# Top-32 attention and a leaky-ReLU block: the softmax division moved from the weights to the transposed values

## The chip, the cores and the metric

The kernel runs on one core of one Trainium2 chip. The metric is device time in microseconds of one execution; smaller is better. Before the change it is 1467.62 us, the median of three runs (1466.69 to 1473.15).

The engines have short names in the profile: PE is TensorE's matmul and PEld its weight load, DVE is VectorE, ACT is ScalarE, POOL is GpSimd, SP is SyncE, which here only issues DMAs. Each engine works through its own instructions in order and waits at semaphores for the others.

## The reference

The shapes are 8 batches, 8 heads, 576 positions, head size 64, all float32; then 4608 tokens, model width 512, hidden width 2048.

```python
scores = scale * np.matmul(q, k.transpose(0, 1, 3, 2))
kth = np.partition(scores, -32, axis=-1)[..., -32:-31]
scores = np.where(scores >= kth, scores, -1e9)
attn = np.exp(scores - np.max(scores, axis=-1, keepdims=True))
attn = attn / (np.sum(attn, axis=-1, keepdims=True) + 1e-09)
x = matmul(attn, v) laid out as (tokens, heads * head size)
h = x @ w_in
out = np.maximum(0.01 * h, h) @ w_out
```

## The kernel before, in words

**Units and steps.** Attention is cut into 144 units. A whole unit is 128 query rows of one pair of heads; its scores are a tile `s_sb` of 128 x 2 x 576 (row, head of the pair, key). Because 576 is 4 x 128 + 64, there are also left units: 64 rows of two pairs of heads each. The main loop (L742) runs over steps `s`; step `s` finds the top 32 of unit `s` on DVE and does the later stages of the units before it. DVE's work for a unit (`top_k`, L295) is two L302 instructions (pairwise maxima and minima), eight L307 (`max`, eight largest at a time) and six L312 (`match_replace`), and is issued in slots between the other engines' work.

**What a unit goes through.** PE computes scores for the two units of steps `s + 2` and `s + 3` at the end of every even step (`scores`, L214) into two PSUM tiles `wide` and one `narrow`, and ACT copies them to `s_sb` (L238, four copies). After the unit's top 32, `limits` (L316) makes two small vectors on ACT and POOL (L322 to L324), `mask` (L326) and `exponents` (L330) run on ACT, two instructions each, in place; the exponentials add up their row sums `z`. `sums` (L334) adds 1e-9 on ACT, `reciprocals` (L338) takes the reciprocal on DVE, between two slots of the next unit's rounds, and `normalize` (L342) multiplies the weights by it on ACT, in place. All of this is in step `n + 1` for unit `n`.

**Transposing.** In step `n + 2`, `transpose` (L345) splits the float32 weights into their two 16-bit halves on POOL (L352, two copies), stores each half to DRAM (L353) and reads both back with one transposing DMA (L355) into `wT`, of which there are three. For units named in `HASTY` (the first eight, 14 and 15), PE transposes nine blocks instead (L365), and ACT copies them out (L371), also in step `n + 2`.

**Values.** `weigh_whole` (L394, 40 matmul instructions for two units) and `weigh_left` (L406) multiply V by `wT`. `values_at` (L622) says when: the two units of a pair of steps together, in the middle of step `(n|1) + 3`, or one step earlier for hasty ones. The result is already transposed: rows are head size, columns are tokens. `keep_values` (L413) copies it with ACT (L418) to the tiles `x`, of which two sets exist.

**The second block.** Tokens go through it in chunks: two of 128 (chunks 0 and 1, `plain`, L573) and 17 of 256 (`mlp`, L491). A chunk of 256 takes 8 steps to become ready. For each, PE makes `ph` (L510) in eight groups, ACT applies the leaky ReLU to `gT` (L516), and PE makes seven products `pz` (L526), with sums and differences of blocks on POOL (L467) that stand in for an eighth product; ACT copies the results to `o_sb` (L533). Two PSUM tiles `ml` serve all of it.

**The order around the change.** Everything is issued in an order written out by hand in the loop at L742. The chunk's work is a generator; `mlp_steps(budget)` (L601) runs it seven times a step until the budget is used up. A matmul's cost is its number of columns. `slot_budget` (L648) divides the work that is waiting by the slots until the step at which the next chunk becomes ready. `sum_now` (L465) issues waiting sums on POOL, `send_now` (L472) stores results through SP. SP's queue holds, in order: loads of Q, K and V, stores of results, and for each unit the two stores and the transposing DMA. `KEPT` names twelve units whose scores are computed in the first steps (`keep_scores`, L273), stored to DRAM and fetched later. Before the loop, the weights, stored as float64, are rounded to float32 on the chip (some 60 us).

Of the kernel before, what the change touches and what calls it, by code (L numbers as in the profile page):

```python
# [9 lines left out]
F32 = mybir.dt.float32  # L10
# [10 lines left out]
def kernel(  # L21
# [192 lines left out]
    def scores(us):  # L214


        narrow = ps_sc.tile([P, 2, 512], F32, name="narrow")
        ps = {}
        for k, u in enumerate(us):
            wide = ps_sc.tile([P, 2, 512], F32, name="wide", bufs=2)  # L220
            ps[u] = ((wide[:, :, 0:WIDE], 0, WIDE),
                     (narrow[:, :, k * NARROW:(k + 1) * NARROW], WIDE, S))

        order = ((us[0], 0), (us[0], 1), (us[1], 1), (us[1], 0))
        for u, part in order:
            to, k0, k1 = ps[u][part]
            for n in range(0, len(u.quarters), 4):
                for i, pi, side, r0, q0 in u.quarters[n:n + 4]:
                    qt, kt = qk_of[pi]
                    d = slice(side * D, (side + 1) * D)  # L230
                    nc.tensor.matmul(to[r0:r0 + LEFT, i, :], qt[d, q0:q0 + LEFT],  # L231
                                     kt[d, k0:k1], start=True, stop=True)
        for u in us:
            u.both = work.tile([P, 2, S], F32, name="s_sb", bufs=5)
            u.s = [u.both[:, i, :] for i in range(2)]
        for u, part in order:
            to, k0, k1 = ps[u][part]
            nc.scalar.copy(u.both[:, :, k0:k1], to)  # L238
# [77 lines left out]
    def limits(u):  # L316
# [4 lines left out]
        u.z = small.tile([P, 2], F32, name="z")  # L321
# [12 lines left out]
    def sums(u):  # L334
        u.ze = small.tile([P, 2], F32, name="ze")
        nc.scalar.activation(u.ze, u.z, AF.Copy, bias=1e-9, scale=1.0)

    def reciprocals(u):  # L338
        u.rz = small.tile([P, 2], F32, name="rz")
        nc.vector.reciprocal(u.rz, u.ze)  # L340

    def normalize(u, i):  # L342
        nc.scalar.activation(u.s[i], u.s[i], AF.Copy, bias=0.0, scale=u.rz[:, i:i + 1])  # L343
# [69 lines left out]
    def keep_values(pair, po, b, q0):  # L413
        ch, col = x_at(b * S + q0)
        if ch not in x_of:
            x_of[ch] = [xpool.tile([P, CHMAX], F32, name=f"x{c}") for c in range(HP)]
        for side in range(2):
            nc.scalar.copy(x_of[ch][pair % HP + side][:, col:col + po.shape[-1]], po[:, side, :])  # L418
# [6 lines left out]
    def hidden_of_few(ch, x):  # L425

        g_of = {}
        for j in range(NFC // 4):
            ph = ps_ml.tile([P, 512], F32, name="ph", tag="ml")
            for c in range(HP):  # L430
                nc.tensor.matmul(ph, x[c][:, 0:P], w_in[c][:, j * 512:(j + 1) * 512],  # L431
                                 start=(c == 0), stop=(c == HP - 1))
                if c == 1:
                    yield 2 * 512
# [56 lines left out]
    def mlp(ch):  # L491
# [13 lines left out]
        for f0 in range(HALF):  # L505
            ph = ps_ml.tile([P, 2, CHMAX], F32, name="ph", tag="ml")
            for i in range(2):
                f = f0 + i * HALF
                for c in range(HP):
                    nc.tensor.matmul(  # L510
                        ph[:, i, 0:n], w_in[c][:, f * P:(f + 1) * P], x[c][:, 0:n],
# [107 lines left out]
    HASTY = (*range(8), 14, 15)  # L619
    MIDDLE, END = 0, 1  # L620

    def values_at(n):  # L622

        return (n | 1) + LAG - (n in HASTY), MIDDLE

# [3 lines left out]
    EARLY_SCORES = {0: 4, 1: 2, 2: 1, 3: 2, 4: 1, 5: 2}  # L629
# [12 lines left out]
    def attended(*place):  # L642
# [5 lines left out]
    def slot_budget(s):  # L648
# [5 lines left out]
        return backlog[0] / ((until + 1 - s) * SLOTS)  # L654

    EARLY_SHARE = 500
    SLOTS = 7

    with tc.manual_schedule():
# [65 lines left out]
        def values(*place):  # L725
# [3 lines left out]
            po = ps_sc.tile([P, 2, 512], F32, name="wide", bufs=2)  # L729
# [7 lines left out]
        def keep(weighed, *place):  # L737
            for u, po in weighed:
                keep_values(u.pairs[0], po, u.b, u.q0)
            attended(*place)  # L740

        for s in range(len(steps) + LAG + 1):  # L742
            assert s < 7 or not to_keep
            cur, old, older, new = unit(s), unit(s - 1), unit(s - 2), ()
            in_haste = s - 2 in HASTY
# [10 lines left out]
            slot()  # L756
            load_waiting()
            send_now()
            if old:
                limits(old)  # L760
            if older and not in_haste:
                transpose(older)
# [3 lines left out]
            if older and in_haste:  # L766
                transpose_in_haste(older)
            if old:
                mask(old, 1)
            slot()  # L770
            if older and in_haste:
                keep_transposed(older)
            mlp_steps(budget)
            if old:
                exponents(old, 0)
            weighed = values(s, MIDDLE)
            if old:
                exponents(old, 1)
                sums(old)
            keep(weighed, s, MIDDLE)  # L780
            if s == 7:
                sum_weights()
            sum_now(3)
            mlp_steps(budget)
            slot()
            if s % 2:
                slot()
            if old:
                reciprocals(old)
            mlp_steps(budget)  # L790
            if old:
                normalize(old, 0)
                normalize(old, 1)
            mlp_steps(budget)
            slot()
            slot()
            if unit(s + 3) in early_units:
                fetch_scores(unit(s + 3))
            mlp_steps(budget)
            if new:  # L800
                scores(new)
            score_early(EARLY_SCORES.get(s, 0))
            budget = slot_budget(s + 1)
            mlp_steps(budget)
# [64 lines left out]
```

## Time and profile before

| what | value |
|---|---|
| median of three runs | 1467.62 us |
| the profiled execution's own time | 1463.53 us |
| its span, first to last instruction | 1461.8 us |
| busy: PE / PEld | 1373.3 us (94%) / 1065.6 us (73%) |
| busy: DVE / ACT / POOL | 1317.9 us (90%) / 1058.5 us (72%) / 728.6 us (50%) |
| DMA | 232.19 MB in 384,445 packets, 320,944 of them under 512 B |
| mean granted clock of TensorE | 0.982 |

The span is what the views below divide. A view by groups gives, for a line and an operation, the count, the busy time, the mean duration of one, and the idle time before it with what ended it. A view of waits sums the idle time by who waited for whom. The chain of waits follows back from the last instruction through whatever released each step. A view by stretches gives busy time per engine in a window of the span. PE's matmuls overlap in the pipeline: the mean duration of one L510 matmul is 383 ns, but 40 of them in a row take 8.83 us, 0.22 us each.

### The profile page before, as it was taken

The numbers are of one execution on the slowest core, as the hardware profiler recorded it, in microseconds if no ns is written. First come the engines' busy times: TensorE is split into PE (matmuls) and PEld (weight loads), VectorE is DVE, ScalarE is ACT, GpSimd is POOL, SyncE is SP. The second block draws the span as 40 slices with busy tenths as digits, with TensorE's granted clock in tenths as the row PEclk, the third lists the DMA queues.
The fourth block names the chain that finished last, engine by engine and source line by source line (L and its number), as shares of the span: only waits on it lengthen the run. The fifth ranks groups of instructions, "written<-read, shape, count | busy, mean of one in ns | idle before, by whom it ended". The sixth has DMA issues, their size and how long they took to land.

```text
span 1461.8 us, 27967 instructions
## 1 busy us (share of the span) xinstructions
PE 1373.3 (94%) x9848; PEld 1065.6 (73%) x9850; DVE 1317.9 (90%) x3401; ACT 1058.5 (72%) x2235; POOL 728.6 (50%) x775
## 2 busy tenths in 40 slices
PE   7858988789999999999999999999899999999998
PEld 2335446668787788878788877778788888788887
DVE  7987899999999999999999999999899999999700
ACT  8887777668687878777778786768587877777711
POOL 3213333554646465555556564556465655555622
PEclk9989998999999999999999999999999999999999
DMA  8941154655666546664766557755766455545420
GB/s 328 343 163 50 57 137 117 180 166 141 198 171 173 141 135 190 189 175 137 211 167 180 145 143 190 190 161 151 191 168 174 130 165 143 164 138 145 131 63 15
DMA packets 384445, 232.19 MB, mean 159 GB/s; under 512 B 320944, under 2 KB 331696, under 8 KB 382384
## 3 DMA queue, kind: packets, MB, share of 16 engines
q1 hardware_dynamic: 383728, 229.88, 55.7%
q8 instruction: 77, 1.26, 0.4%
q14 instruction: 64, 0.52, 0.1%
q10 hardware_dynamic: 576, 0.52, 0.1%
HBM read 55.77 MB, written 95.55 MB: 104 GB/s over the span
## 4 chain that ended last, share of the span: by engine, by line
PE 65%; DVE 18%; DMA 7%; ACT 6%; issue 2%; POOL 2%; SPq 0%; ACTq 0%; DVEq 0%; POOLq 0%
PE ph L510 23%; PE pz L526 22%; PE wide L394 9%; DVE tops L307 8%; DVE pairs L312 6%; PE wide L231 4%; DMA wT<-apart 4%; PE narrow L231 2%; PE pz L578 2%; DVE pairs L302 2%; DMA apart<-split 2%; ACT s_sb L238 1%; PE ph L431 1%; DMA vt<-in_vk_dram 1%; ACT s_sb L331 1%
## 5 line engine op out<-in xcount | busy, mean ns | idle before, releaser
L307 DVE MAX8 tops<-pairs 128x8 f32<-128x288 f32 (+1 forms) x1152 | 638.5, 595 | 0.0
L510 PE MATMUL ph<-x,w_in 128*128 128x256 f32 x2176 | 491.7, 383 | 1.6 <-ACT gT L516 1.6
L510 PEld LDWEIGHTS ph<-x,w_in 128*128 128x128 f32 x2176 | 407.4, 190 | 84.0 <-issue 20.8
L312 DVE MATCH_REPLACE8 pairs<-tops,pairs 128x288 f32<-128x288 f32 (+1 forms) x864 | 461.5, 541 | 0.0
L323 POOL TENSOR_TENSOR nbias<-tops 128x2 f32<-128x2 f32 x144 | 107.9, 749 | 574.5 <-DVE tops L307 567.1
L352 POOL COPY split<-s_sb 128x1152 uint16<-128x1152 uint16 x268 | 298.7, 1143 | 8.3 <-ACT s_sb L343 8.3
L343 ACT ACTIVATE s_sb<-s_sb,rz 128x576 f32<-128x576 f32 x288 | 207.3, 768 | 66.9 <-DVE rz L340 66.7
L526 PE MATMUL pz<-w_out,gT 128*128 128x256 f32 x1088 | 245.2, 381 | 0.6 <-ACT o_sb L533 0.6
L526 PEld LDWEIGHTS pz<-w_out,gT 128*128 128x128 f32 x1088 | 205.7, 190 | 31.5 <-issue 2.5
L331 ACT ACTIVATE s_sb<-s_sb,nbias 128x576 f32<-128x576 f32 x288 | 219.3, 764 | 0.9
L328 ACT ACTIVATE s_sb<-s_sb,nleast 128x576 f32<-128x576 f32 x288 | 214.4, 770 | 4.7
L302 DVE TENSOR_TENSOR pairs<-s_sb 128x576 f32<-128x576 f32 x288 | 212.3, 778 | 5.0
L394 PE MATMUL wide<-wT,vt 128*64 128x128 f32 (+1 forms) x2560 | 165.4, 290 | 30.2 <-DMA wT<-apart 21.5
L394 PEld LDWEIGHTS wide<-wT,vt 128*64 128x64 f32 (+1 forms) x2560 | 134.6, 141 | 68.1 <-issue 31.3
L238 ACT COPY s_sb<-wide 128x704 f32<-128x704 f32 x130 | 98.1, 755 | 86.4 <-PE wide L231 86.4
L516 ACT ACTIVATE gT<-ph 128x512 f32<-128x512 f32 x136 | 80.5, 592 | 76.7 <-PE ph L510 76.7
L526 PE MATMUL pz<-raw,top 128*128 128x256 f32 x544 | 125.0, 384 | 0.0
L526 PEld LDWEIGHTS pz<-raw,top 128*128 128x128 f32 x544 | 101.1, 190 | 21.2 <-issue 8.4
L231 PE MATMUL wide<-kt,qt 64*64 64x352 f32 x1040 | 105.0, 474 | 3.6 <-ACT wT L371 2.9
L324 POOL TENSOR_SCALAR nbias<-nbias 128x2 f32<-128x2 f32 x144 | 85.8, 596 | 12.6
L418 ACT COPY x<-wide 128x128 f32<-128x128 f32 (+1 forms) x160 | 32.2, 260 | 74.4 <-PE wide L394 57.9
L533 ACT COPY o_sb<-pz 128x256 f32<-128x256 f32 x119 | 43.8, 368 | 57.1 <-PE pz L526 57.1
(81 smaller groups left out, 1202.1 us busy)
## 6 DMA issues: line engine op xcount, KB each, us to landing
apart<-split SPq DMA_DIRECT2D x268, 288.0 KB, 2.2
raw<-in_weights_dram SPq DMA_DIRECT2D x15, 1024.0 KB, 6.9
vt<-in_vk_dram SPq DMA_DIRECT2D x32, 320.0 KB, 3.9
qt<-in_qT_dram SPq DMA_DIRECT2D x32, 288.0 KB, 3.8
kt<-in_kT_dram SPq DMA_DIRECT2D x32, 288.0 KB, 3.9
out_dram<-o_sb SPq DMA_DIRECT2D x68, 128.0 KB, 3.0
kept<-gT SPq DMA_DIRECT2D x12, 576.0 KB, 4.3
s_sb<-kept SPq DMA_DIRECT2D x12, 576.0 KB, 4.3
```

The costliest lines, as they stand in the source:

```text
L231: nc.tensor.matmul(to[r0:r0 + LEFT, i, :], qt[d, q0:q0 + LEFT], kt[d, k0:k1], start=True, stop=True)
L238: nc.scalar.copy(u.both[:, :, k0:k1], to)
L302: nc.vector.tensor_tensor(pairs[:, :, n, :], u.both[:, :, 0:HS], u.both[:, :, HS:S], op)
L307: nc.vector.max(out=u.tops[:, i, r, :], in_=rest[i])
L312: nc.vector.match_replace(out=rest[i], in_to_replace=u.tops[:, i, r, :], in_values=rest[i], imm_value=LOWEST)
L328: nc.scalar.activation(u.s[i], u.s[i], AF.Prelu, bias=u.nleast[:, i:i + 1], scale=1.0, alpha=BELOW)
L331: nc.scalar.activation(u.s[i], u.s[i], AF.Exp, bias=u.nbias[:, i:i + 1], scale=SCALE, accum_out=u.z[:, i:i + 1])
L343: nc.scalar.activation(u.s[i], u.s[i], AF.Copy, bias=0.0, scale=u.rz[:, i:i + 1])
L352: nc.gpsimd.tensor_copy(split, pairs[:, :, h])
L394: nc.tensor.matmul(po[n * D:(n + 1) * D, side, 0:P], v_of[u.pairs[0]][k, at, side, :], u.wT[k, at + side * NKC if at + 1 < NKC else at, :] ...
L510: nc.tensor.matmul(ph[:, i, 0:n], w_in[c][:, f * P:(f + 1) * P], x[c][:, 0:n], start=(c == 0), stop=(c == HP - 1),)
L526: nc.tensor.matmul(to, g[:, f, :], w(f), start=(first and f == 0), stop=(f == HALF - 1), skip_group_check=not first)
```

## The change

The weights are no longer divided by their sums. The unnormalized exponentials are transposed and multiplied with V, and the transposed values are multiplied by the reciprocals. Since their columns are tokens, each reciprocal has to stand in a column and to be repeated over the 64 partitions of its head. So two units' sums are taken together, 1e-9 is added, and DVE takes reciprocals of a 128 x 4 tile; a DMA stores them transposed in DRAM, other DMAs read them back spread over 64 partitions each, and POOL multiplies `x` in place after ACT's copy.

Three things move. The split, or the hasty transpose, is in the step of the unit's own exponentials instead of the step after. Scores for the coming pair are in the middle of an even step directly behind the values, which use a spare part of the scores' first PSUM tile; hasty values are at the start of their step. `sum_now(3)` comes before the masks. Units 142 and 143 become hasty, the early scores are spread differently over the first five steps, and the budget of chunk work takes 2800 columns off every even step.

```diff
+    def in_order(us):
+        return (us[0], 0), (us[0], 1), (us[1], 1), (us[1], 0)
...
-    def sums(u):
-        u.ze = small.tile([P, 2], F32, name="ze")
-        nc.scalar.activation(u.ze, u.z, AF.Copy, bias=1e-9, scale=1.0)
-    def reciprocals(u):
-        u.rz = small.tile([P, 2], F32, name="rz")
-        nc.vector.reciprocal(u.rz, u.ze)
-    def normalize(u, i):
-        nc.scalar.activation(u.s[i], u.s[i], AF.Copy, bias=0.0, scale=u.rz[:, i:i + 1])
+    def sums(n):
+        z = z_of[n].rearrange("p n i -> p (n i)")
+        z_of[n, "e"] = ze = small.tile([P, 4], F32, name="ze")
+        nc.scalar.activation(ze, z, AF.Copy, bias=1e-9, scale=1.0)
+    def reciprocals(n):
+        rz = small.tile([P, 4], F32, name="rz")
+        nc.vector.reciprocal(rz, z_of[n, "e"])
+        over[n] = halves.tile([4, P], F32, name="over")
+        nc.sync.dma_start(over[n].rearrange("k t -> t k"), rz)
+    def spread(n):
...
+            for k in range(2):
+                nc.sync.dma_start(to[k * D:(k + 1) * D, :, :],
+                                  over[n][2 * k:2 * k + 2, :].partition_broadcast(D))
...
-        for side in range(2):
-            nc.scalar.copy(x_of[ch][pair % HP + side][:, col:col + po.shape[-1]], po[:, side, :])
+        to = x_of[ch][:, pair % HP:pair % HP + 2, col:col + po.shape[-1]]
+        nc.scalar.copy(to, po)
+        return to
...
-    HASTY = (*range(8), 14, 15)
+    HASTY = (*range(8), 14, 15, 142, 143)
...
-        return (n | 1) + LAG - (n in HASTY), MIDDLE
+        return ((n | 1) + 2, START) if n in HASTY else ((n | 1) + LAG, MIDDLE)
...
-    EARLY_SCORES = {0: 4, 1: 2, 2: 1, 3: 2, 4: 1, 5: 2}
+    EARLY_SCORES = {0: 4, 1: 2, 2: 2, 3: 2, 4: 2}
...
-        return backlog[0] / ((until + 1 - s) * SLOTS)
+        group = [GROUP * (at % 2 == 0 and at < len(steps)) for at in range(s, until + 1)]
+        return max((backlog[0] + sum(group)) / len(group) - group[0], 0.0) / SLOTS
...
+        def divide(weighed):
+            for k, (x, place) in enumerate(weighed):
+                first = [n for n in range(len(steps)) if values_at(n) == place][0]
+                nc.gpsimd.tensor_tensor(x, x, over[first][k], ALU.mult)
```

The step's body after the change, in order (the diff replaces nearly all of it):

```python
            for _ in range(6):
                slot()
            load_waiting()
            send_now()
            if s % 2 and s - 3 in z_of:
                spread(s - 3)
            if old:
                limits(old, s - 1)
            sum_now(3)
            weighed = values((s, START))
            if old:
                mask(old, 0)
            mlp_steps(budget)
            if old:
                mask(old, 1)
            mlp_steps(budget)
            ps, spare = tiles_for_scores(new) if new else (None, None)
            if not weighed:
                weighed = values((s, MIDDLE), spare)
            if new:
                scores(new, ps)
            if old:
                exponents(old, 0)
                exponents(old, 1)
                if s % 2 == 0:
                    sums(s - 2)
            place = (s, s % 2 == 0)
            kept_x = keep(weighed, place)
            if new:
                keep_scores_of(new, ps)
            if old and not in_haste:
                transpose(old)
            divide(kept_x)
            attended(place)
...
            for _ in range(5):
                mlp_steps(budget)
            if old and in_haste:
                transpose_in_haste(old)
                keep_transposed(old)
            if unit(s + 3) in early_units:
                fetch_scores(unit(s + 3))
            if old and s % 2 == 0:
                reciprocals(s - 2)
            score_early(EARLY_SCORES.get(s, 0))
            load_more(s)
```

## The prediction

> **What bounds the kernel now.** I read the page's slices first: from slice 9 on, PE and DVE both stand at 9 tenths, ACT at 7 to 8, POOL at 4 to 6. So I asked for busy time by stretches of 100 us.
>
> ```profile
> 250.00:300.00 50.00, 42.65 (x394) 34.84 (x393) 44.82 (x119) 35.78 (x81) 26.26 (x28) 0.93 0.61 169
> 900.00:1000.00 100.00, 96.58 (x774) 78.78 (x773) 95.53 (x251) 74.31 (x165) 54.41 (x59) 1.00 0.64 173
> 1100.00:1200.00 100.00, 100.00 (x734) 80.50 (x734) 99.18 (x259) 76.24 (x167) 55.45 (x60) 1.00 0.54 149
> ```
>
> Columns: stretch, its length, then busy us of PE, PEld, DVE, ACT and POOL, the granted clock, DMA share, GB/s. At its best (third line) PE has no gap at all and DVE almost none; elsewhere both lose 3 to 5 us in 100 together. The kernel is paced by PE with DVE one per cent behind, and what can be won is their common gaps. The waits say what opens them:
>
> ```profile
> DVE rz L340 <- ACT ze L336: 49.7, 25, 8.2
> PE wide L394 <- DMA wT<-apart: 21.5, 11, 5.4
> PE wide L406 <- DMA wT<-apart: 5.6, 2, 4.5
> PE wide L406 <- DMA vt<-in_vk_dram: 5.1, 4, 1.8
> PE ph L510 <- ACT gT L516: 1.6, 2, 1.0
> ```
>
> (total us, times, longest.) DVE's stalls are nearly all one wait: the reciprocal of a unit stands between DVE's rounds of the next, and waits for the sum that ACT makes after its exponentials. PE's stalls after 300 us are nearly all one too: the values wait for a transposed tile that was started only one step before. ACT waits on PE (86.4 us before the scores' copies, 76.7 before gT), so it follows PE.
>
> How much a gap costs is read from the chain of waits, by the first L510 block of each chunk of tokens:
>
> ```profile
> 401.21 8.83 PE ph L510 x40
> 457.63 5.80 DMA wT<-apart
> ...
> 761.23 8.83 PE ph L510 x40
> ...
> 832.12 8.83 PE ph L510 x40
> ...
> 1268.45 8.83 PE ph L510 x40
> ...
> 1339.34 8.83 PE ph L510 x40
> ```
>
> A chunk that meets no wait takes 832.12 - 761.23 = 70.89 us, and 1339.34 - 1268.45 gives the same 70.89: that is PE's floor. The 13 chunks from 401.21 to 1339.34 took 938.1 us, 72.16 each. The timeline puts chunk 2's first L510 at 237.16 and the last chunk's at 1405.5; from there to the end are 56.3 us. So the span is 237.2 + 1168.3 (16 periods) + 56.3 = 1461.8. DVE's own floor is its step of 8.78 us without a wait (L302 at 1059.54 and 1068.32), 70.2 per chunk of 8 steps.
>
> **The change, part by part.**
>
> *Normalization leaves ACT.* 288 x 0.72 us = 207.3 us (L343) go; the sums go from 144 to 72 (14.7 us); the copies of the values become 64 of 128x256 (0.37 us, as L533) and 16 small ones, some 4 us less; two more pairs of L371 copies add 2.5. ACT falls from 1058 to about 835 us. By itself worth nothing in mid-kernel, where ACT follows PE; it counts before 240 us, where the timeline shows ACT without a gap for long stretches (71 to 74 us, 82 to 90, 101 to 110).
>
> *Reciprocals.* 72 of 128x4 instead of 144 of 128x2 save 72 x 0.15 = 11 us on DVE: a step of 8.70, 69.6 per chunk. More matters that they stand behind all rounds of an even step, and need a sum that ACT makes a third of a step earlier than the rounds end. The 49.7 us should go; what is late next is PE, at 70.89 per chunk.
>
> *Split one step earlier.* A unit's GpSimd copies, two stores and transpose move from step n+2 to the middle of step n+1, behind its own exponentials; the values stay at (n|1)+3. The later unit of a pair gains more than half a step, some 5 us, against waits of at most 5.4. I cost the 27.1 us of waits for wT at 27.1 saved. The values also get faster: 40 matmuls after a wait took 4.31 us (317 us) or 3.67 (390 us) against 2.35 without one, so about 1.5 us more per long wait is in the periods above.
>
> *Values next to scores.* On PE this reorders 2.35 + 2.1 us per two steps and takes one switch away; I cost it at nothing. On ACT the four score copies (2.5 us) follow the copy of the values instead of ending the step. Queued behind them are gT copies; PE has two ph banks of 1.77 us each to go on with. The same block of copies stands before MLP work today and PE lost 1.6 us on gT in all. Cost 0; if the cover fails, 0.5 us per pair, 36 us.
>
> *Division on POOL.* 64 products of 128x256 at 0.73 us (the o_sb sums, L467) and 16 of 128x128, at most 0.73: 47 to 58 us, less four split copies (4.6). POOL goes from 729 to about 780 of 1462, while it waits 567 us for tops today. The cost is latency. In program order the new chunk's first ph stands behind the values (2.35), the scores (2.1) and 16 pz matmuls (16 x 0.22 = 3.5): 5.6 us after the values end. In that time ACT copies (0.4), POOL ends the split copies (2 x 1.14, begun when the exponentials end) and multiplies (0.73). By my layout the product comes 1.5 to 2.3 us before PE asks. Cost 0; uncovered 2 us per chunk. In chunk 2, ph follows the values directly: the product then comes about 8.4 us into the step (store and spread 3 us each, copies and product the rest) against 4.7 now, +3.7 once.
>
> A rule weighed: the Trainium skill, "GPSIMD Engine Reference", section 4.1, puts two-input elementwise work on VectorE and calls GpSimd about twice as slow. The rows agree on the size (L302's 128x576 takes 0.78 us, POOL's 128x256 0.73), but DVE has 1 us in 100 free and POOL 45, so by the rule some 25 us would join the bound.
>
> *Reciprocals through DRAM.* 72 stores of 128x4 as 4-byte pieces, and 160 spreading loads, all on SP. No row shows a store of such pieces. Price of a packet today: 1461.8 x 16 x 0.557 / 383,728 = 34 ns. If 16 engines share 512 pieces, 32 x 34 ns = 1.1 us over the 2.2 us landing of L353, so 3.3; if one engine takes all, 17.4 + 2.2 = 19.6. I take 3.3, since the transposes' packets, also small, land in 4.6 us at some 2,400 each. SP waits at the spread with the next split stores behind it; those come about 5 us into the step, so 3.3 us is covered. The product is asked for nearly two steps after the reciprocal, about 16.8 us, so nothing is late below some 13 us of landing.
>
> A rule weighed: the Trainium skill, "DMA: Bandwidth & Descriptors", section "Rules for kernel authors", says that a strided last dimension becomes one descriptor per element and should be made contiguous. It speaks against this store; no run yet shows it.
>
> *The last pair in haste.* 18 PE transposes at 15.2/90 = 0.17 us: +3.0 us; the store, transpose and their waits (1.3 us in the last period) go. *Budget.* The new budget gives the even step less MLP work; the total is the same: 0.
>
> **Sum.** Before chunk 2, DVE took 187.1 us for 19 steps (60.7 to 247.8) against 19 x 8.78 = 166.8: 20.3 us of stalls, with ACT full. Normalization is 19 x 1.44 = 27 us of that ACT time. Bounds 0 and 20.3; I take 14, since the copies of early scores (12 units x 1.2 us) stay; with the 3.7 this gives -10.3. Periods: 15 x 70.9 + (66.2 - 1.3 + 3.0) = 1131.4. Waits that remain: bounds 0 and 27; I take 8, the waits above that have nothing to do with wT (5.1 + 1.6 and small ones). Span: 237.2 - 10.3 + 1131.4 + 8 + 56.3 = 1422.6. The profiled execution stood 1.7 us above its span and the median 4.1 above that: **1428**.
>
> **Rivals.**
> 1. *Half a gain* (0.20): early, PE's and ACT's work on early scores sets the pace and nothing is won (240.9), and 12 us of waits remain: 1440.6, or 1446. For it: long PE waits there are for gT copies of early scores (8.3 us). Against: ACT is full there.
> 2. *The product becomes the wait that wT was* (0.13): POOL is a queue, and split copies wait on ACT ahead of the product. If it comes 2 us late at 17 chunks, 34 us are lost: 1462, no change. Against: POOL is half idle.
> 3. *Slower* (0.12): the 4-byte store lands late. Place: SP, at the spread; it decides from about 13 us of landing. At 14 us each of 72 pairs loses 1 us: 1500; at the upper end 19.6, some 6 us per pair, 1830. Against: the 34 ns above.
> 4. Forecast (0.55): 1409 to 1441.
>
> That the change doesn't do what it says I exclude: the built program has 72 fewer DVE, 436 fewer ACT, 76 more POOL and 226 more SP instructions, as counted here.
>
> No change means within 0.5%, about what measurement can tell: 1460.3 to 1475. Faster: cases 4 and 1 and a third of 2, 0.79; same 0.09; slower 0.12. The range takes in 4 and 1 with part of the bounds: 1409 to 1458.
>
> **What would show it.** Right: no DVE wait at the reciprocal, no PE wait for wT, chunk periods of 70.9, chunk 2 starting near 227. Wrong: PE waiting at L546's ph for POOL; SP waiting over 8 us at the spread; POOL's product after the time PE asks; early steps as long as now. The largest unknown is the early gain.

## The result, and the profile after

The changed kernel takes **1949.64 us**, median of four runs (1941.64 to 1954.65), against 1467.15 us for the kernel before (four runs, 1464.95 to 1473.15): a ratio of 1.3275, 95% interval 1.3215 to 1.3335. It is slower by a third, where 1428 us was forecast. The profiled execution took 1948.64 us with a span of 1946.8.

The stretches of the changed kernel (stretch, length, busy PE, PEld, DVE, ACT, POOL, granted clock, DMA share, GB/s):

```profile
900.00:1000.00 100.00, 75.67 (x491) 60.95 (x489) 71.06 (x180) 38.99 (x87) 35.33 (x45) 0.89 0.57 125
1100.00:1200.00 100.00, 76.32 (x522) 61.09 (x523) 64.99 (x161) 42.41 (x94) 38.55 (x51) 0.88 0.49 120
```

No engine is full any more. PE, which had no gap from 1100 to 1200 us before, is idle a quarter of the time, DVE a third. Less is done too: 522 matmul records instead of 734. PE's granted clock fell from 1.00 to 0.88 in that stretch, and its busy time over the whole span rose from 1373.3 to 1503.1 us though its work is nearly the same. When all engines have gaps, the pace is set by something that the table of busy time doesn't list. The chain of waits, summed by line over the changed kernel's span, names it:

```profile
DMA over<-rz 19%; PE ph L546 13%; DMA apart<-split 12%; DVE tops L314 5%; SPq L390 5%; PE pz L562 5%; DVE pairs L319 4%; POOL split L387 3%; SPq L367 2%; PE wide L429 2%; DMA wT<-apart 2%; PE wide L236 2%; DVE pairs L309 1%; ACT s_sb L342 1%; POOL x L782 1%
```

`over<-rz` is the new store of the reciprocals, 2 KB at a time: 19% of the span, about 370 us, stand at it, and another 12% at the stores of the halves, `apart<-split`. The waits of the changed kernel say who stands there (total us, times, longest):

```profile
POOL split L387 <- DMA apart<-split: 854.8, 100, 18.6
DVE rz L355 <- ACT ze L348: 357.7, 58, 13.5
ACT s_sb L342 <- POOL nbias L335: 342.8, 84, 9.0
...
PE wide L429 <- DMA wT<-apart: 109.5, 33, 6.8
```

The wait at the reciprocal, 49.7 us before, is 357.7 now; ACT's wait for the limits (`nbias`), of which before showed next to nothing, is 342.8; PE's waits for `wT` went from 27.1 to 109.5 us at L429 alone. The greatest is new: POOL waits 854.8 us because the stores of the halves haven't emptied its two `split` buffers. The same view for SP alone:

```profile
SPq L367 <- DMA over<-rz: 442.6, 52, 11.0
SPq L390 <- DMA apart<-split: 398.7, 140, 5.7
SPq L376 <- DMA over<-rz: 67.7, 8, 9.3
...
```

At the spread (L367, L376) SP stands 442.6 + 67.7 = 510 us. One pair of steps on SP's timeline (start us, us, queue, line, transfer):

```profile
1008.07 0.57 SPq L357 DMA_DIRECT2D over<-rz  x1
1008.69 0.50 SPq L182 DMA_DIRECT2D vt<-in_vk_dram  x1
1018.38 1.10 SPq L367 DMA_DIRECT2D scale<-over  x2
1019.60 1.13 SPq L388 DMA_DIRECT2D apart<-split  x2
1023.27 2.60 SPq L390 DMA_TRANSPOSE wT<-apart  x1
...
1027.54 0.99 SPq L388 DMA_DIRECT2D apart<-split  x2
1031.57 2.43 SPq L390 DMA_TRANSPOSE wT<-apart  x1
1034.05 0.58 SPq L357 DMA_DIRECT2D over<-rz  x1
```

From a store to the spread that reads it are 10.3 us (over all 72 pairs: 8.2 to 11.6, median 9.4), and from there to the next store 15.7: 26.0 us for a pair of steps, where 70.89/4 = 17.7 was PE's floor. The queue is a loop of its own: each part of it waits for the landing of the one before, and none for PE or DVE for long.

What stands behind it follows from POOL's timeline at the same place. The split copies at 1022.42 us had waited 14.0 us for `apart<-split`; the product of the values (1025.00) and the next unit's limits, `nbias` (1025.68), are behind them in POOL's queue. So ACT's exponentials start late, the sum after them too, and the reciprocal at 1012.67 us, the last thing on DVE in its step, had waited 12.5 us. Even so SP is later than DVE: the store of that reciprocal is the one at 1034.05 us, 21.4 us after it (over all 72 pairs 21.5 in the median), and the store at 1008.07 holds the reciprocals of 982.62. The delay runs from SP through POOL and ACT to DVE and PE.

### The profile page after: what moved, and what is told of

It reads as the page before. It is cut to its first block, busy times and chain, and to the rows that moved or that the text cites. A ratio compares the mean times of both kernels' runs of the same rounds, so it can differ in the third digit from the quotient of the medians.

```text
span 1946.8 us, 28034 instructions
## 1 busy us (share of the span) xinstructions
PE 1503.1 (77%) x9868; PEld 1161.6 (60%) x9868; DVE 1355.7 (70%) x3329; ACT 842.9 (43%) x1799; POOL 674.3 (35%) x851
## 3 DMA queue, kind: packets, MB, share of 16 engines
q1 hardware_dynamic: 430320, 237.12, 49.7%
## 4 chain that ended last, share of the span: by engine, by line
DMA 37%; PE 25%; DVE 13%; SPq 10%; issue 7%; POOL 6%; ACT 3%; ACTq 0%; POOLq 0%; DVEq 0%
DMA over<-rz 19%; PE ph L546 13%; DMA apart<-split 12%; DVE tops L314 5%; SPq L390 5%; PE pz L562 5%; DVE pairs L319 4%; POOL split L387 3%; SPq L367 2%; PE wide L429 2%; DMA wT<-apart 2%; PE wide L236 2%; DVE pairs L309 1%; ACT s_sb L342 1%; POOL x L782 1%
## 5 line engine op out<-in xcount | busy, mean ns | idle before, releaser
L387 POOL COPY split<-s_sb 128x1152 uint16<-128x1152 uint16 x264 | 303.4, 1178 | 1019.9 <-DMA apart<-split 854.8
L546 PE MATMUL ph<-x,w_in 128*128 128x256 f32 x2176 | 524.0, 402 | 92.3 <-POOL x L782 74.8
L546 PEld LDWEIGHTS ph<-x,w_in 128*128 128x128 f32 x2176 | 434.0, 202 | 184.5 <-POOL x L782 80.0
L342 ACT ACTIVATE s_sb<-s_sb,nbias 128x576 f32<-128x576 f32 x288 | 220.0, 765 | 342.9 <-POOL nbias L335 342.8
L309 DVE TENSOR_TENSOR pairs<-s_sb 128x576 f32<-128x576 f32 x288 | 255.9, 929 | 140.1 <-ACT s_sb L245 102.5
L429 PE MATMUL wide<-wT,vt 128*64 128x128 f32 (+1 forms) x2560 | 208.3, 329 | 114.4 <-DMA wT<-apart 109.5
L562 PE MATMUL pz<-w_out,gT 128*128 128x256 f32 x1088 | 262.4, 400 | 39.5 <-ACT o_sb L569 38.0
L429 PEld LDWEIGHTS wide<-wT,vt 128*64 128x64 f32 (+1 forms) x2560 | 166.8, 163 | 160.1 <-DMA wT<-apart 101.0
L355 DVE RECIPROCAL rz<-ze 128x4 f32<-128x4 f32 x72 | 12.5, 173 | 357.7 <-ACT ze L348 357.7
L453 ACT COPY x<-wide 128x256 f32<-128x256 f32 (+1 forms) x80 | 27.2, 351 | 315.7 <-PE wide L236 290.2
L236 PE MATMUL narrow<-kt,qt 64*64 64x224 f32 x1040 | 71.4, 377 | 49.5 <-DMA kt<-in_kT_dram 49.5
L782 POOL TENSOR_TENSOR x<-x,scale 128x256 f32<-128x256 f32 (+1 forms) x80 | 58.4, 735 | 119.2 <-DMA scale<-over 83.1
L441 PE MATMUL wide<-wT,vt 128*64 128x64 f32 x640 | 31.8, 270 | 87.7 <-DMA vt<-in_vk_dram 86.1
```

Of the source, the lines that this page charges most:

```text
L309: nc.vector.tensor_tensor(pairs[:, :, n, :], u.both[:, :, 0:HS], u.both[:, :, HS:S], op)
L342: nc.scalar.activation(u.s[i], u.s[i], AF.Exp, bias=u.nbias[:, i:i + 1], scale=SCALE, accum_out=u.z[:, i:i + 1])
L387: nc.gpsimd.tensor_copy(split, pairs[:, :, h])
L429: nc.tensor.matmul(po[n * D:(n + 1) * D, side, 0:P], v_of[u.pairs[0]][k, at, side, :], u.wT[k, at + side * NKC if at + 1 < NKC else at, :] ...
L546: nc.tensor.matmul(ph[:, i, 0:n], w_in[c][:, f * P:(f + 1) * P], x[:, c, 0:n], start=(c == 0), stop=(c == HP - 1),)
L562: nc.tensor.matmul(to, g[:, f, :], w(f), start=(first and f == 0), stop=(f == HALF - 1), skip_group_check=not first)
```

## The experiments

Chunk 2 starts at 253.8 us now, 16 periods take 1637.4 (102.3 each), and the tail is 55.6. The loss lies in the periods, all over the kernel. Theory S: SP's wait at the spread is the loss, since everything behind it in SP's queue is late. Rivals: the slow store holds other transfers too, whether SP waits or not; or the moved steps or POOL's product are to blame, and the store is a symptom.

Kernels with one run have no interval. Single runs of the kernel before lie up to 0.7% from their median. What is read from a kernel with one run is more than that, except for e8's own +10 us (0.7%).

### e1_rows16: the store in 16-byte pieces

```diff
-        nc.sync.dma_start(over[n].rearrange("k t -> t k"), rz)
+        nc.sync.dma_start(over[n].rearrange("k t -> (k t)").rearrange("(t k) -> t k", k=4), rz)
```

> The store of the reciprocals keeps its place, size and readers, but goes to DRAM in 128 pieces of 16 bytes instead of 512 of 4, so the reciprocals are divided into the wrong columns. Theory S (SP is the bound: its queue holds 15.5 us of work per two steps before, had 408/72 = 5.7 us free, and now stands 9.4 us at the spread; the length comes from the 4-byte pieces, (9.4 - 2.2)/32 = 0.22 us each per engine): landing 2.2 + 8 x 0.22 = 4 us, wait at the spread under 4 us, time 1430 to 1500. Rival Q (the store is slow because of its place behind the transposing DMA or of DRAM, not of its pieces): landing stays 8 to 10, time about 1950. Rival P (POOL's queue: splits and product ahead of the limits, whatever SP does): time above 1800.

Measured: 1520.55 us (one run; before, on the same chip, 1468.51). It is a little over the 1500 that theory S allowed. The store lands in 2.4 us; SP still waits at L367, 62 times, 112.3 us in all. The reciprocals end up in the wrong columns, but the same work is done. One line about how a 2 KB tile is stored takes 429 of the 482 us away. So the store's layout is the cause of most of it, and the moved steps and the product, which are all still there, are not.

### e2_spread_late: the spread at the end of the odd step

```diff
-            if s % 2 and s - 3 in z_of:
+            if s % 2 and s - 3 in z_of and s - 3 in HASTY:
                 spread(s - 3)
...
+            if s % 2 and s - 3 in z_of and s - 3 not in HASTY:
+                spread(s - 3)
             if unit(s + 3) in early_units:
```

> All of the change, but for pairs that are not hasty the spread is issued at the end of the odd step, behind that step's split stores and transpose, not at its start. The store keeps its 4-byte pieces. Theory S: landing stays 8 to 11 us, but SP has work of its own meanwhile, so the wait at the spread falls below 3 us and the time to 1420 to 1480. Rival P: the split stores were not what mattered, and the spread comes later, so POOL's product comes later still: 1950 or more. Rival D (the small writes slow every other DMA by contention): transposes and stores still land late, time above 1600.

Measured: 1939.46 us, ratio 1.3238 (1.3172 to 1.3304). Nothing is won, though SP's wait at the spread fell from 510 to 58.4 us. Its waits and a piece of its timeline in this kernel:

```profile
SPq L390 <- DMA apart<-split: 886.3, 140, 13.5
```

```profile
1024.35 0.53 SPq L357 DMA_DIRECT2D over<-rz  x1
...
1026.00 0.90 SPq L388 DMA_DIRECT2D apart<-split  x2
1037.54 2.43 SPq L390 DMA_TRANSPOSE wT<-apart  x1
```

The stores of the halves are issued 1.65 us after the reciprocals' store, but the transposing DMA that waits for them starts only 10.6 us after their issue ended. The wait has changed its place, not its size. Theory S fell: SP need not wait for the store to suffer from it. The late place has a price of its own, though: POOL's product waits 314.5 us for the spread here, so this run alone doesn't say what the store costs; e7 does.

### e3_no_route: everything but the route

Store and spread are gone; POOL multiplies by a piece of `w_in`, so the division is left out of what is computed, and its cost on POOL is kept.

```diff
-        over[n] = halves.tile([4, P], F32, name="over")
-        nc.sync.dma_start(over[n].rearrange("k t -> t k"), rz)
...
+        any_of = w_in[0][:, 0:2 * P].rearrange("p (i t) -> p i t", i=2)
...
+            over[n] = [any_of]
```

> All of the change without the store and the spreading loads: POOL multiplies by a tile that is there anyway, so the softmax sums are not divided out. Everything else, the reciprocals too, stays. Theory S: what the forecast was made of is all that is left, 1410 to 1450, no wait of SP for the reciprocals, PE's chunk period near 70.9 us. Rival P: still above 1700.

Measured: 1439.25 us, ratio 0.9816 (0.9777 to 0.9855). This is the forecast's kernel without its route, 0.8% from the forecast. The best stretch in it:

```profile
1100.00:1200.00 100.00, 96.15 (x720) 78.48 (x723) 99.38 (x255) 57.48 (x128) 56.67 (x64) 0.97 0.53 143
```

DVE is full, PE 4 us short of it. The route costs 1946.8 - 1436.9 = 510 us of span, 7.1 per pair, and all the rest of the change gains 25 (29 by the medians).

### e5_before_plus_route: the kernel before, with the route

The kernel before divides as it did; four reciprocals of a pair are also stored and spread, and nobody uses them.

```diff
+    def store(n):
+        over[n] = halves.tile([4, P], F32, name="over")
+        nc.sync.dma_start(over[n].rearrange("k t -> t k"), rz_of[n])
...
+            if s % 2 and s - 3 in over:
+                spread(s - 3)
```

> The kernel before, with only the route added: the reciprocals of two units in one 128x4 tile, stored in 4-byte pieces at the end of the even step and read back spread at the start of the odd one; nobody uses the result. Theory S: the wait at the spread, 8 to 11 us, takes SP over its free 5.7 us per two steps, and the time rises by 300 to 700 us, to 1770 to 2150, POOL's splits waiting for the stores. Rival P (the loss comes from the new order and the product): no more than 5% slower, below 1540.

Measured: 2001.05 us (one run), +533. SP waits 549.0 us at the spread. Without the rest of the change the route's price is about the same, 533 against 510.

### e7_store_alone and e8_store_apart: one store, two layouts

Both are e5 without the spread, so no instruction waits for the store. In e7 it is the change's store. In e8 each 4-byte piece lies 64 bytes from the next:

```diff
-        over[n] = halves.tile([4, P], F32, name="over")
-        nc.sync.dma_start(over[n].rearrange("k t -> t k"), rz_of[n])
+        over[n] = halves.tile([4, P, 16], F32, name="over")
+        nc.sync.dma_start(over[n].rearrange("k t w -> t k w")[:, :, 0:1], rz_of[n].rearrange("p (k w) -> p k w", w=1))
```

> The kernel before, with only the store of two units' reciprocals in 4-byte pieces added, at the end of the even step on SP; nothing is read back, so nobody ever waits for it. Theory R or E (the pieces delay the DMAs behind them): SP waits for split stores and PE for wT, time 1700 to 2000. Theory S as first held (only SP's waiting at the spread costs): no wait is added, time within 2% of before, 1460 to 1500.

> As the run with the store alone, but in DRAM the 4-byte pieces stand 64 bytes apart, so that no two share 64 bytes. If the cost is that of a piece as such (0.2 us each per engine): same time as with the store alone, within 3%. If it comes from neighbouring pieces that are written into the same few bytes by different engines: near the kernel before, 1460 to 1520.

Measured: e7 1856.65 us, e8 1476.93 (one run each; before 1466.92). Both move the same 422,463 packets. SP's timeline in e7:

```profile
1018.06 0.52 SPq L349 DMA_DIRECT2D over<-rz  x1
1021.65 2.06 SPq L369 DMA_DIRECT2D apart<-split  x2
1030.51 2.55 SPq L371 DMA_TRANSPOSE wT<-apart  x1
```

and in e8:

```profile
1024.15 0.53 SPq L349 DMA_DIRECT2D over<-rz  x1
1024.91 1.42 SPq L369 DMA_DIRECT2D apart<-split  x2
1028.15 2.75 SPq L371 DMA_TRANSPOSE wT<-apart  x1
```

The same pair of stores is waited for until 12.5 us after the reciprocals' store in e7, and until 4.0 us after it in e8, where the reciprocals land in 2.4 us. Over the kernel SP's wait before the transposing DMA is 833.2 against 331.9 us. So a store that nobody waits for costs 390 us, and the number of its pieces isn't why: the same number, apart, costs 10, which is within what single runs differ by. What costs is that the pieces are **neighbours**: 16 of them in each 64 bytes, written one by one.

The packets show whose time it is. The profile lists, for SP's DMA queue, packets, MB and the time that the packets took as a share of 16 engines' span; first e7, then e8:

```profile
q1 hardware_dynamic: 421744, 230.04, 70.6%
q1 hardware_dynamic: 421744, 230.04, 56.8%
```

The 4-byte packets aren't the slow ones: in the traces they take 9 ns in the median in both kernels. The packets of 2,304 bytes, most of them the stores of the halves, take 249 ns on average in e7 (at most 9.1 us) and 102 in e8 (at most 1.3 us). The neighbouring pieces are paid for by other transfers.

### e11_store_grouped: four pieces in 64 bytes

```diff
-        over[n] = halves.tile([4, P], F32, name="over")
-        nc.sync.dma_start(over[n].rearrange("k t -> t k"), rz_of[n])
+        over[n] = halves.tile([P, 8, 2], F32, name="over")
+        nc.sync.dma_start(over[n][:, 0:4, 0:1], rz_of[n].rearrange("p (k o) -> p k o", o=1))
```

> As the run with the store alone, on the kernel before: 4-byte pieces again, but each row of 128 has its four pieces 8 bytes apart in a place of its own of 64 bytes, so that only the pieces of one row share 64 bytes. If pieces hold each other up within 64 bytes whoever writes them, four in a row cost a part of what sixteen cost: 1500 to 1750. If only pieces of different rows do: as with the pieces 64 bytes apart, 1465 to 1490.

Measured: 1508.28 us (one run; before 1469.92); the store lands in 3.3 us. The four pieces of one row, 8 bytes apart, now share 64 bytes, and no two rows do. That gives a series for the store alone, at 512 pieces each:

| pieces in the same 64 bytes | kernel | cost | landing |
|---|---|---|---|
| 1 | e8 | +10 us | 2.4 us |
| 4 (of one row) | e11 | +38 us | 3.3 us |
| 16 (of 16 rows) | e7 | +390 us | 8.2 to 11.6 us (in the changed kernel, to the spread's issue) |

Sharing 64 bytes isn't enough by itself: in e1 four pieces of 16 bytes, from four rows and 128 in all, share them too and land in 2.4 us.

### e6_store_on_act: the store from ACT's queue

e2, with the store issued by ACT. If the stores of the halves waited only for their turn in SP's queue, this would free them.

```diff
-        nc.sync.dma_start(over[n].rearrange("k t -> t k"), rz)
+        nc.scalar.dma_start(over[n].rearrange("k t -> t k"), rz)
```

> The late spread, and the store of the reciprocals issued by ACT instead of SP, so that it stands in another DMA queue; still 512 pieces of 4 bytes. What the run with the late spread showed: SP no longer waits at the spread, but the split stores issued behind the reciprocals' store land 11 us late. Theory R (the pieces hold up only what stands behind them in the same DMA queue): the split stores land in 2 to 4 us again, time 1440 to 1500. Theory E (the pieces hold the DMA engines themselves, whatever queue they come from): stores and transposes still land late, 1750 to 1950.

Measured: 1914.25 us (one run), against e2's 1939. The store lands in 11.7 us; the stores of the halves, from SP, land in 4.2 (median; 2.2 before), and SP waits for them up to 13.6 us, 749.5 in all. The median alone would not show much, since the late spread is in this kernel too: in e9 below, with a late spread too but a quick store, it is 3.8. But there SP waits 442.1 us for these stores, at most 7.1, and no packet of 2,304 bytes takes over 1.2 us, against 9.7 here. So the place in SP's queue isn't what holds them: a store from another queue does it too. The Trainium skill, "DMA: Bandwidth & Descriptors", section "Issuing engines are not separate DMA queues", says that DMAs from different issuing engines run on the same 16 DMA engines, and that spreading them saves issue time only. The run agrees: 25 of some 480 us.

### e9_dve_turned, e14_turned_between, e16_turned_few: rows turned on DVE

If neighbouring pieces are the cause, the reciprocals should be turned into rows on the chip before they are stored. DVE's transpose of 32x32 blocks does that in 0.21 us for a 128x32 tile. e9 stores that whole tile (128 pieces of 128 B) and spreads with twice as many loads, at the end of the odd step:

```diff
+        rz = wide_rz[n // 2 % 2]
+        nc.vector.reciprocal(rz[:, 0:4], z_of[n, "e"])
+        turned_rz = small.tile([P, 32], F32, name="rz", bufs=2)
+        nc.vector.transpose(turned_rz, rz)
+        over[n] = halves.tile([P, 32], F32, name="over")
+        nc.sync.dma_start(over[n], turned_rz)
```

> All of the change, same result, with another way for the reciprocals: DVE puts them in a 128x32 tile, transposes it in blocks of 32, and one store writes 128 pieces of 128 bytes; the spreading loads read pieces of 128 bytes, four or eight loads per pair, late in the odd step. Theories R and E alike (the trouble is the number of small pieces): landing 2 to 4 us, no wait at the spread, time 1435 to 1475, at best that of the run without the route (1439) and some us for 2.2 us of issue on SP per pair. If instead any trip through DRAM in SP's queue costs as much, over 1500.

Measured: 1618.00 us, ratio 1.1039 (1.1006 to 1.1072), over 1500 as the rival said, but for another reason. The store is cured (it lands in 2.2 us), but POOL's product now waits for the spread, 323.0 us (61 times, at most 17.6): behind the odd step's transposing DMA, which itself waits, the spread is too late. e14 issues it between the odd step's stores of halves and its transposing DMA:

```diff
-    def transpose(u):
+    def transpose(u, between):
...
             nc.sync.dma_start(apart[:, h, :], split)
+        between()
         u.wT = work.tile([P, 2 * NKC - 1, P], F32, name="wT", bufs=3)
```

> The route with DVE's transpose and pieces of 128 bytes again (1618 with the spread at the end of the odd step), but the spreading loads stand between that step's split stores and its transposing DMA. Theory L (the late loads were the trouble: POOL's product waited 323 us for them, and the limits of the next unit stand behind it in POOL's queue): product no longer waits, 1455 to 1490. Rival M (1,024 more pieces of 128 bytes per pair slow the other DMAs and SP, wherever they stand): above 1550.

Measured: 1495.90 us, ratio 1.0189 (1.0152 to 1.0226), between the two expectations. The place was worth 122 us, but the product still waits 92.2 us, and the spread lands in 4.3 us. e16 stores only the four rows that hold reciprocals, as whole rows of 512 B in DRAM, and goes back to the change's spread, with half the loads and 1 KB read by each partition:

```diff
-        over[n] = halves.tile([P, 32], F32, name="over")
-        nc.sync.dma_start(over[n], turned_rz)
+        over[n] = halves.tile([4, P], F32, name="over")
+        for b in range(4):
+            nc.sync.dma_start(over[n][:, 32 * b:32 * b + 32], turned_rz[32 * b:32 * b + 4, :])
```

> All of the change, same result: DVE turns the reciprocals in blocks of 32, but only their four rows are stored, by four small stores of 4 x 128 bytes (16 pieces per pair), the spreading loads read rows as in the change (128 pieces of 1 KB, two loads), and they stand between the odd step's split stores and its transposing DMA. If pieces and SP's waits are what costs: the 1453 of the 16-byte pieces, plus 72 x 0.21 = 15 us on DVE if DVE sets the pace, plus some 1 us of issue on SP per pair: 1453 to 1475, level with the kernel before or a little faster. If the run with pieces of 128 bytes (1496) was slow for DVE's transpose and not for its 1,024 pieces, then again 1485 to 1500.

Measured: **1453.05 us**, median of six runs (1450.85 to 1458.76), against 1468.72 (eleven runs): ratio 0.9896 (0.9867 to 0.9925). It beats both kernels. SP's waits in it:

```profile
SPq L398 <- DMA apart<-split: 222.2, 129, 4.6
SPq L395 <- POOL split L394: 209.8, 167, 8.1
```

and PE's:

```profile
PE wide L449 <- DMA vt<-in_vk_dram: 26.4, 5, 8.4
PE narrow L236 <- DMA kt<-in_kT_dram: 10.2, 3, 4.2
```

At the spread SP waits 13.1 us in all, and it has time to spare again: 209.8 us in which it waits for POOL's copies. PE has lost its waits for `wT`; the two greatest of what is left are late loads of V and K. The route now costs 1453 - 1439 = 14 us. DVE's transpose is the same in e14 and e16, so the 43 us between them come from store and spread; whether from the number of pieces or from twice as many spreading loads in SP's queue isn't separated.

### e15_rows16_between: the place without the turn

e1's store with e14's place for the spread (the reciprocals end up in the wrong columns, as in e1).

> The store in 128 pieces of 16 bytes (reciprocals in the wrong columns, 1521 with the spread at the start of the odd step), with the spreading loads between the odd step's split stores and its transposing DMA. Theory S, what is left of it (SP's wait of 1.8 us at the spread and 62 such waits made the difference to 1439): 1440 to 1470. Rival (16-byte pieces in the same 64 bytes still hold the DMAs behind them): 1500 or more.

Measured: 1453.10 us (one run; before 1468.76), 67 less than e1. With a quick store, SP's wait at the spread is what is left to pay, and the place lowers it from 112.3 to 37.7 us; SP waits for POOL's copies 229.6 us instead of 62.3, so it has time to spare again.

### e10_spread_by_pe and e13_turned_rows: PE instead of the DMA

e10 spreads without any DMA: PE multiplies an identity by each column of reciprocals, broadcast over 64 columns, and ACT copies the result. e13 uses PE only to turn the 128x4 tile into four rows, which are stored and spread as in e15.

```diff
+        def row(at, k, t0, t1):
+            nc.tensor.matmul(at, rz[:, k:k + 1].to_broadcast([P, D]), ident[:, t0:t1],
+                             start=True, stop=True)
```

> All of the change, same result, but the reciprocals are spread without any DMA: in the odd step PE multiplies the identity by each column of the 128x4 reciprocals, taken 64 times, into PSUM (4 matmuls of 128 columns per pair), and ACT copies the result to SBUF for POOL's product. Theory (the route through DRAM is all that was wrong): 1439 of the run without the route, plus 4 x 0.11 = 0.44 us or half of it on PE for 72 pairs: 1450 to 1475, no DMA wait of POOL's product, no wait of SP added. If the product on POOL itself were a burden, the run without the route would have shown it; above 1500 the theory is wrong.

```diff
+    def turn(n):
+        ps = ps_sc.tile([P, 2, 512], F32, name="narrow")[0:4, 0, 0:P]
+        nc.tensor.matmul(ps, over[n], ident, start=True, stop=True)
+        rows = small.tile([4, P], F32, name="rows", bufs=1)
+        nc.scalar.copy(rows, ps)
```

> All of the change, same result, with a route that writes few pieces and is never waited for: in the odd step PE turns the 128x4 reciprocals into 4x128 with one product with the identity (0.16 us, a quarter of what the spread by PE took), ACT copies it, SP stores four rows of 512 bytes, and the spreading loads stand between that step's split stores and its transposing DMA, where SP waits for the split stores anyway. Theory (small pieces in the same 64 bytes, and after them SP's and PE's time, were all that was wrong): 1439 of the run without the route, 12 us of PE, and up to 15 us for 1.6 us of issue on SP per pair: 1445 to 1466, a little faster than the kernel before. If it is slower than 1475, the change's own gain does not survive any route that was tried.

Measured: e10 1492.73 us, ratio 1.0171 (1.0133 to 1.0209); e13 1488.73, ratio 1.0145 (1.0098 to 1.0192). Both are slower than expected. In e10 PE's work for the spread is 47.5 us (0.66 per pair, 0.44 expected), put on an engine that has nothing to spare. In e13 PE's part is 27.5 us (0.38 per pair, 0.16 expected), and there are new handovers: ACT waits 68.4 us for PE's rows and SP 119.7 for ACT's. How much of the 49 us over e3 each of them costs isn't separated.

### e12_acts_normalize: the order alone

The change's order of steps, with the division back on ACT, in the step of the exponentials, before the split. POOL takes the reciprocal as a power; the 1e-9 is left out, and product and route are gone.

```diff
+        nc.gpsimd.tensor_tensor(u.rz, u.z, minus_one, ALU.pow)
...
+    def normalize(u, i):
+        nc.scalar.activation(u.s[i], u.s[i], AF.Copy, bias=0.0, scale=u.rz[:, i:i + 1])
```

> The change's order alone: split in the exponentials' step, values next to scores, new budget, hasty last pair; but the weights are divided by ACT before the split, as in the kernel before, with a reciprocal that POOL makes (power of -1, without the 1e-9, which float32 loses beside sums of at least 1). No product on the values, no route. If the gain of the run without the route comes from the order (earlier split, DVE freed of the wait for the sum): 1430 to 1465. If it comes from relieving ACT (207 us of normalization, back now): no gain, 1460 to 1500. The price of POOL's power on 128x2 is not shown by any row; it adds to the chain from exponentials to split.

Measured: 1554.56 us, ratio 1.0577 (1.0547 to 1.0608); neither expectation met. ACT waits 99.2 us for POOL's powers (0.81 us each) and POOL 245.3 us for ACT's sums, so a new exchange between the two stands in the step. This exchange costs more than either gain, so the run doesn't answer its question: what the order gains beside the move of the division isn't separated.

## Why the prediction was wrong

**The step that failed is "Reciprocals through DRAM".** It took 3.3 us for the landing, from 34 ns for a packet spread over 16 engines. That is the price of an average packet, and the landing doesn't follow from it: the 4-byte packets take only 9 ns each by the trace, and still it took 8.2 to 11.6 us until the reader could start. My upper end, 19.6, held it; I took the lower value because the transposes' packets, also small, land in 4.6 us, that is, by size and count, without a look at where the pieces lie. e8 shows that for pieces that lie apart even 3.3 was too much (2.4).

**The cover was read too generously.** "SP waits at the spread with the next split stores behind it; those come about 5 us into the step, so 3.3 us is covered" took SP to be free until then. "Nothing is late below some 13 us of landing" counted from the reciprocal to the use of the product, 16.8 us, as if the store started at once. A row of the kernel before, which I didn't use, says how free SP is:

```profile
SPq L353 <- POOL split L352: 407.9, 258, 40.9
```

SP's time to spare was its wait for POOL's copies: 407.9 us, over 72 pairs 5.7 us each. So a pair takes 17.7 - 5.7 = 12.0 us of SP's loop. The spread starts 9.4 us after the store's issue and takes 1.1 to issue, which makes an estimated 22.5, 4.8 over the 17.7 of a pair, or some 350 us. Measured are 7.1 per pair (510 us). SP's wait for the stores of the halves grew from 314.5 to 398.7 us, 1.2 per pair more. What makes up the rest isn't separated; PE's clock, 0.88, is among the candidates: 38 matmuls of the values after a wait of 5.46 us took 3.74 us, against 2.35 for 40 without a wait. In the changed kernel SP waits for POOL's copies 14.4 us in all: nothing is to spare. The 16.8 us from the reciprocal to its use are gone before the store starts, since it stands 21.5 us behind the reciprocal in SP's queue.

**A path was missed.** I looked at who waits for the store. e2, e6 and e7 show that transfers which don't depend on it are late too.

**Rival 3 had the place and the cause, and a wrong threshold.** "The 4-byte store lands late. Place: SP, at the spread" is what the trace shows; "it decides from about 13 us" is not. At its own price, 1 us per pair at 14 us of landing, it would have said no loss at the 9.4 that was measured. Its evidence against, "the 34 ns above", was the wrong row. The sign named for being wrong, "SP waiting over 8 us at the spread", came: 442.6 us in 52 waits, 8.5 each. The rule weighed there (one descriptor per element) pointed the right way, but its reason, the count, is not what costs here: e7 and e8 have the same count. The Trainium skill, "DMA: Bandwidth & Descriptors", section "Specifications", says that a transfer under 512 B is done as a read-modify-write. That would suit neighbours that have to wait for each other, but no run here shows what happens inside, and by size alone e8 would be as slow as e7.

**The other steps** are judged by e3, the change without its route:

- Bound: right that PE and DVE set the pace within 4% of each other, wrong in the order: in e3 DVE is ahead (99.38 of 100 us). DVE's busy time didn't fall by the 11 us of the reciprocals, it is 1321.1 after 1317.9: the maxima and minima on DVE (L302, L309 in e3) average 819 ns instead of 778, 12 us in all. Of the 15 that overlap with POOL's product in e3, 11 took over 800 ns, where the median of all is 757. The 16 periods took 1158.4 us; I had 1131.4 + 8.
- ACT to 835 us: right, 842.9 in the changed kernel and 839.4 in e3.
- The reciprocal's waits (49.7 us) should go: 22.2 are left in e3. PE's waits for `wT` (27.1): gone in e3.
- Values next to scores at no cost: no wait in e3 speaks against it.
- The product on POOL at no cost: right for PE, which waits once for it to start a chunk of 256 in e3, 4.3 us, where +3.7 was forecast for chunk 2. With the route, 74.8 us.
- The early gain, 14 - 3.7 = 10.3 us: chunk 2 starts at 222.9 us in e3, forecast 226.9. Too small by 4.
- Waits that remain, 8 us: too small. PE's loads of V and K alone are 31.2 in e3.
- The last pair in haste, +3.0: not measured by itself. The tail is 55.6 us in both; I had 56.3.

Summed, the forecast's span without the route would have been 1422.6 against e3's 1436.9, 1% off, partly because a gain taken too small offsets waits taken too small; the route was off by 510.

What stays open: why neighbouring small writes are slow, and whether the limit is 64 bytes or another length, since from e7 through e11 to e8 the pieces also get sparser over any longer stretch. A third `split` buffer, which might loosen POOL from SP's queue, wasn't tried.

## What to carry to other kernels

Before a DMA that waits is put into a queue, read how much time that queue has to spare, which is the time it waits for its own producers, and set the landing against that, not against the moment at which the result is needed. Turn a column of per-partition scalars into rows on the chip before it is stored (32x32 blocks on DVE, 0.21 us), and put the load that reads it back where its queue waits anyway. A transfer of 2 KB can cost a third of a kernel: judge one by how its pieces lie in memory, not by its bytes or by the mean price of a packet.

## What the runs showed of the hardware

- A store of 512 pieces of 4 bytes, 16 neighbours to 64 bytes and each from another partition, takes 8.2 to 11.6 us until its reader can start. With each piece in its own 64 bytes it lands in 2.4 us, with four of one row in 64 bytes in 3.3.
- While such a store runs, stores issued after it land late, from the same queue or another: SP waits for them up to 13.5 us in e7 and 13.6 in e6, 4.5 before. The time isn't in the 4-byte packets, 9 ns each, but in the others: those of 2,304 bytes take 249 ns on average in e7, 102 in e8.
- With more gaps PE had a lower granted clock: busy 94% of the span at 0.982 before, 87% at 0.936 in e9, 80% at 0.900 in e7, 77% at 0.878 in the changed kernel, where nearly the same matmuls were busy 130 us longer.
